# Four small reorderings in a linear-attention and token-mixer kernel: the opening's statistics and transposes, one fill and one sum in the first mixer, one sum in the second

## The chip, the cores and the metric

The kernel runs on one core of one Trainium2 chip. The metric is the device time of one execution in microseconds (us), lower is better. A ratio is the mean time of one kernel's fast runs over the mean of the other's fast runs of the same rounds, so it is not quite the ratio of the medians quoted beside it.

## The reference, cut to what matters

```python
x = A_x                                            # 2048 tokens x 1024, bf16
h  = x + linear_attention(layernorm(x), wqkv, wo)  # 32 heads of 32
h2 = h + mixer(layernorm(h), w1, b1, w2, b2)       # per feature: 2048 -> 3584 -> gelu -> 2048
```

Three stretches matter here. In the **opening** the first four tiles of 128 tokens are loaded, normalised, transposed on TensorE and multiplied with the key weights. The **first mixer** is the product with w1, the **second mixer** that with w2. Both mixers are computed with seven half-size products in place of eight (a Strassen-like scheme, applied twice: seven outer products "p1" to "p7", some of them split again into seven inner ones "i1" to "i7"). The scheme costs many sums and differences of operands on VectorE and copies on ScalarE; TensorE's stream is meant never to wait for them. Each mixer goes through its outputs in **quads**, four tiles of 128 at a time; "in2", "in3" and "in5" are the inner blocks of p2, p3 and p5, and "hi", "wq", "e" are tiles that VectorE's sums write.

## The kernel before

The order on each engine is mostly the order of the program. The opening, with lines that the change doesn't touch cut:

```python
pin(ln[0][1](0)); warm_up(2, ...)      # statistics of tile 0, first half; warm-up matmuls
pin(ln[0][1](1)); pin(ln[0][2]())      # second half, aggregate
warm_up(2, ...)
stats(0)                               # ScalarE: 1/sqrt(var)
norm_halves(0)                         # VectorE: normalise tile 0
transpose_in(0)                        # TensorE: 2 x 4 transposes; ScalarE: 2 copies 128x512
ln_stats(1); stats(1)                  # statistics of tile 1
k_unit(0, 0)                           # 8 products 128x512 with key weights
norm_halves(1); transpose_in(1)
ln_stats(2); stats(2); k_unit(1, 0); norm_halves(2)
# ... k_unit(0, 1), transpose_in(2), ln_stats(3), stats(3)
phi_dve((0, 0))
w_sums(kmov, slice(0, 1))              # VectorE: 1.22 us sum of weights
norm_halves(3)
# ... k_unit(1, 1)
transpose_in(3)
```

Both mixers weave the seven inner products with steps of an outer one; each stretch of such steps is a **fill**:

```python
def interleave(self, n, steps, at={}, flush=...):
    t = len(steps)
    cuts = [0, (5*t+8)//16, (9*t+8)//16, (12*t+8)//16, t]
    for f in (n.i1, "b", 0, n.i6, "c", n.i2, "2", 1, n.i5, n.i7, "7", 2, n.i3, "third", 3, n.i4, "end"):
        ...   # a number: that share of the steps; a string: flush late ScalarE work, run at[name]
```

An inner block keeps two halves, b and c (and a and e), of PSUM banks. In the second mixer b and c are halves of one bank. i7 adds into c and VectorE then reads c; i3 adds into b. In the second mixer the sums for p7 stood together ahead of the block:

```python
self.asums(7)                          # two sums wq<-wq, one for each of the pair
self.interleave(self.in5, self.steps(*[st.p6 for st in sts]))
third_sums()                           # only in the first quad: four more sums
```

Of the kernel before, what the change touches and what calls it, by code (L numbers as in the profile page):

```python
# [30 lines left out]
def kernel(  # L31
# [62 lines left out]
    def warm_up(n, behind=None):  # L94
        def mm(lhsT, rhs):
            ps = warm_tiles[0]
            warm_tiles.append(warm_tiles.pop(0))
            pin(nc.tensor.matmul(ps[0:lhsT.shape[-1], 0:rhs.shape[-1]], lhsT=lhsT, rhs=rhs, start=True, stop=True))

        if behind is not None:  # L100
            mm(behind, behind)
        for t in range(n):
            mm(warm[:, 0:P], warm[:, 0:BANK])
# [395 lines left out]
    class Quad:  # L499
# [27 lines left out]

        late = []

        def interleave(self, n, steps, at={}, flush=(("7", None), ("end", None))):  # L530
            t = len(steps)
            cuts = [0, (5 * t + 8) // 16, (9 * t + 8) // 16, (12 * t + 8) // 16, t]
            flush = dict(flush)

            def fill(q):
                for f, part in groupby(steps[cuts[q]:cuts[q + 1]], lambda s: s[0]):
                    f([k for _, k in part], self.late)

            def point(name):
                todo = len(self.late) if flush.get(name, 0) is None else flush.get(name, 0)  # L540
                for _ in range(todo):
                    self.late.pop(0)()
                at.get(name, nop)()

            for f in (
                n.i1, "b", 0, n.i6, "c", n.i2, "2", 1, n.i5, n.i7, "7", 2, n.i3, "third", 3, n.i4, "end",
            ):
                if isinstance(f, int):
                    fill(f)
                elif isinstance(f, str):  # L550
                    point(f)
                else:
                    f()
# [25 lines left out]
        def run2(self, pend, on_p4, on_p7, cut, third_sums):  # L579
            sts = self.sts  # L580

            def starting():
                self.in1.sums(slice(2, 4))
                self.asums(5)
                self.in5 = self.inner(5)
                self.in5.sums(slice(0, 2))
                sts[0].asum(6)
                for st in sts:
                    st.begin()

            self.interleave(
                self.in1, self.steps(*[st.p4 for st in pend]),
                {"b": starting, "7": lambda: self.in5.sums(slice(2, 4))}, (("b", self.early), ("7", None), ("end", None)),
            )
            sts[1].asum(6)
            on_p4()
            e = share(sts)
            for st in sts:
                st.fetch(1, 1)
            for st in sts:  # L600
                st.fetch(0, 0)
                st.fetch(0, 1)
            self.asums(7)
            self.interleave(self.in5, self.steps(*[st.p6 for st in sts]))
            third_sums()
            self.asums(3)
            in3 = Inner2(sts, 3, self.mov3, "i", self.add_to(e), None)
            in3.sums()
            for st in sts:
                st.p7()  # L610
                dve.tensor_tensor(st.e[:], st.B[:], st.e[:], ALU.add)
            if cut is not None:
                sts[-1].split(cut)
            for st in sts:
                st.fetch(1, 0)
            nxt, halves = on_p7()

            def begin_next():
                if nxt is not None:
                    nxt.in1 = nxt.inner(1)  # L620
                    nxt.in1.sums(slice(0, 2))
                sts[0].evac(0, 1, sts[0].e)

            self.interleave(in3, self.steps(*[st.p2 for st in sts]), {
                "2": halves[0], "7": halves[1], "third": begin_next,
                "end": lambda: self.late.append(lambda: sts[1].evac(0, 1, sts[1].e)),
            }, (("7", None),))
            return sts, nxt
# [43 lines left out]
        def run1(self, pend, nxt, on_p4, third_sums=None):  # L672
            sts = self.sts
            s4, s6, s7 = self.steps(*[st.p4 for st in pend]), self.steps(*[st.p6 for st in sts]), self.steps(*[st.p7_fill for st in sts])
            c6, c7 = 3 * len(s6) // 4, len(s7) // 2

            def starting():
                self.in1.sums(slice(2, 4))
                self.asums(5)
                self.in5 = Inner(sts, 5, self.mov5, "i5", self.sink5, self.sum5)  # L680
                self.in5.sums(slice(0, 2))
                self.asums(6)
                self.t1 = self.base("t1a")
                for s, st in enumerate(sts):
                    st.begin(self.t1[:, s, :])

            def gelu(s, dh, t):
                return lambda: sts[s].evac(0, dh, t[:, s, :])

            def gelu_late(*args):  # L690
                return lambda: self.late.insert(0, gelu(*args))

            self.in1.behind = self.late
            self.interleave(
                self.in1, s4, {"b": starting, "7": lambda: self.in5.sums(slice(2, 4))}, (("b", None), ("7", None))
            )
            self.asums(7)
            in2 = Inner2(sts, 2, self.mov2, "i1", self.add_to(self.t1), None)
            in2.sums()
            on_p4()  # L700
            nxt = nxt()
            share(sts)
            if third_sums is not None:
                third_sums(slice(0, 3))
            self.interleave(self.in5, s6[:c6], flush=(("b", None), ("7", None), ("end", None)))
            sts[0].finish()
            self.asums(3)
            self.base3()
            in3 = Inner2(sts, 3, self.mov3, "i5", self.add_to(self.t3), None)
            in3.sums()  # L710
            sts[0].with_shared(sts[0].base3, sts[0].B)
            self.interleave(
                in2, s6[c6:] + s7[:c7], {"third": gelu(0, 0, self.t1), "end": gelu_late(1, 0, self.t1)}, (("7", None),)
            )
            sts[1].with_shared(sts[1].base3, sts[1].B)
            if nxt is not None:
                nxt.begin1()
            self.interleave(in3, s7[c7:], {
                "7": nop if third_sums is None else lambda: third_sums(slice(3, 4)),
                "third": gelu(0, 1, self.t3), "end": gelu_late(1, 1, self.t3),  # L720
            }, (("b", 1), ("c", None)))
            return sts, nxt
# [13 lines left out]
    with ExitStack() as actx:  # L736
# [21 lines left out]
        with ExitStack() as a1:  # L758
# [28 lines left out]
            def ln_chunks(i, x_sb):  # L787
                st = a1s.tile([P, NDC, nc.vector.BN_STATS_DIM], F32, name="st")
                mv = a1s.tile([P, nc.vector.BN_AGGR_DIM], F32, name="mv")
                lnv = a1s.tile([P, 1], F32, name="lnv")  # L790
                rstd = a1s.tile([P, 1], F32, name="rstd")
                xn = xin.tile([P, D], BF16, name="xn")

                def stats(c):
                    return nc.vector.bn_stats(st[:, c, :], x_sb[:, c * CW:(c + 1) * CW])

                def aggr():
                    return nc.vector.bn_aggr(mv[:], st[:])

                def scale():  # L800
                    yield nc.scalar.activation(lnv[:], mv[:, 1:2], ACT.Ln, bias=eps_ln[:], scale=1.0)
                    yield nc.scalar.activation(rstd[:], lnv[:], ACT.Exp, scale=-0.5)

                def norm(cs):
                    return nc.vector.tensor_scalar(xn[:, cs], x_sb[:, cs], mv[:, 0:1], rstd[:, 0:1], ALU.subtract, ALU.mult)

                return xn, stats, aggr, scale, norm, st, mv
# [264 lines left out]
            def stats(i):  # L1072
                for op in ln[i][3]():
                    pin(op)
# [28 lines left out]
                phis[i, c] = k_parts(i, c)  # L1103

            phis = {}
            warm_up(2, xs[0][:, 0:CW // 8])
            ln[0] = ln_chunks(0, xs.pop(0))
            pin(ln[0][1](0))
            warm_up(2, ln[0][5][:, 0, :])
            pin(ln[0][1](1))  # L1110
            pin(ln[0][2]())
            warm_up(2, ln[0][6][:])
            stats(0)
            norm_halves(0)
            transpose_in(0)
            ln_stats(1)
            stats(1)
            k_unit(0, 0)
            norm_halves(1)
            transpose_in(1)  # L1120
            ln_stats(2)
            stats(2)
            k_unit(1, 0)
# [541 lines left out]
```

## Time and profile before

| | before |
|---|---|
| time, median of 3 runs | 566.08 us (565.63 to 566.12) |
| span of the profiled execution | 564.1 us |
| TensorE busy | 555.1 us (98%) |
| share of the chain of waits that is TensorE | 91% |

The head of the page of the kernel before, and the fourth part of it (the chain that ended last):

```profile
span 564.1 us, 8722 instructions
PE 555.1 (98%) x3262; PEld 310.0 (55%) x3278; DVE 448.3 (79%) x853; ACT 287.4 (51%) x609; POOL 1.8 (0%) x8
...
PE 91%; DVE 6%; ACT 1%; issue 1%; DVEq 0%
```

TensorE is the bound, so only its gaps can be won. The list of TensorE's waits in the kernel before (who waited for whom: us in total, times, longest):

```profile
PE psI L229 <- DVE e L229: 1.9, 3, 0.7
...
PE acc_t L826 <- ACT xnT L1079: 0.9, 2, 0.5
PE psI L229 <- DVE hi L229: 0.4, 1, 0.4
...
```

The opening in the timeline (columns: start, duration, engine, line, operation, written <- read, shape, count; in brackets the idle time before it and what ended it):

```profile
10.50 3.63 PE L826 MATMUL acc_t<-wkv,xnT 128*128 128x512 bf16 x15 [0.46 <-ACT xnT L1079]
...
12.06 1.29 DVE L795 BATCH_NORM_STATS2 st<-x_sb 128x6 f32<-128x512 bf16 x2
...
13.97 0.61 PE L1069 MATMUL tp<-ident,xn 128*128 128x128 bf16 x8
14.20 1.22 DVE L876 TENSOR_TENSOR pqT<-wkv 128x2048 f16<-128x2048 bf16 x1
...
15.92 0.73 DVE L805 TENSOR_SCALAR xn<-x_sb,mv,rstd 128x512 bf16<-128x512 bf16 x2 [0.51 <-ACT rstd L802]
16.39 0.72 PE L1069 MATMUL tp<-ident,xn 128*128 128x128 bf16 x8
```

The product group at 10.50 is tile 1's key unit, which waited for ScalarE's copy (tile 0's, at 7.70, did likewise); the transposes (tp) at 13.97 and 16.39 are tile 2's and tile 3's, 2.42 us apart. Those of tile 3 come right behind tile 3's normalisation; pqT<-wkv is the weight sum.

The first mixer, one quad, in the timeline:

```profile
268.32 0.35 ACT L229 COPY psI<-psI 128x256 f32<-128x256 f32 x1
268.73 0.60 PE L229 MATMUL psI<-hi,is 128*128 128x256 f16 x4
...
272.63 0.60 PE L229 MATMUL psI<-hi,wq 128*128 128x256 f16 x4
...
277.23 0.68 DVE L229 TENSOR_TENSOR hi<-hO,hi 128x1024 f16<-128x1024 f16 x1
...
277.97 0.60 PE L229 MATMUL psI<-hi,sa 128*128 128x256 f16 x4 [0.39 <-DVE hi L229]
```

The product at 268.73 starts just as ScalarE's copy of 268.32 is over; the product at 277.97 waits for the sum "hi".

The second mixer, first of three quads:

```profile
449.54 2.08 DVE L229 TENSOR_TENSOR wq<-wq 128x1792 f16<-128x1792 bf16 x2
...
451.54 0.42 DVE L229 TENSOR_TENSOR e<-psI,es 128x256 f32<-128x256 f32 x1
452.01 0.93 PE L229 MATMUL psI<-gE,is 128*128 128x256 f16 x7 [0.65 <-DVE e L229]
...
452.97 0.42 DVE L229 TENSOR_TENSOR e<-psI,es 128x256 f32<-128x256 f32 x1 [1.01 <-PE psI L229]
```

Both sums wq<-wq run ahead of the addition that the product at 452.01 needs.

### The profile page before, as it was taken

The page shows a single profiled execution, that of the slowest core. Times are in us where ns is not written, and L with a number is a line of the kernel's source. Part 1 is how long each engine was busy: PE and PEld are TensorE (multiplying, and loading weights), DVE is VectorE, ACT ScalarE, POOL GpSimd, SP SyncE. Part 2 cuts the span into 40 slices and gives each one's busy share as a digit, 9 for nine tenths or more (in the row PEclk, how much of TensorE's full clock was granted, in tenths as well). Part 3 has the DMA queues.
Part 4 walks back from the last instruction along what each step waited for, and adds up shares of the span by engine and source line. Part 5 has one row for each costly group of instructions (what it writes and reads, how often), then busy time and mean ns, then how long its engine had stood idle before and what let it go on. Part 6 is the DMA issues. An engine that isn't in the chain of part 4 may idle for free.

```text
span 564.1 us, 8722 instructions
## 1 busy us (share of the span) xinstructions
PE 555.1 (98%) x3262; PEld 310.0 (55%) x3278; DVE 448.3 (79%) x853; ACT 287.4 (51%) x609; POOL 1.8 (0%) x8
## 2 busy tenths in 40 slices
PE   8999999999999999999999999999999999999997
PEld 3444444454444444456666766666445656656654
DVE  6898888544776788889889789888998899869874
ACT  4747777766766877645546465555211313213212
POOL 1000000000000000000000000000000000000000
PEclk9999999999999999999999999999999999999999
DMA  9933342115764861103041340432946643652111
GB/s 303 295 76 75 79 90 39 19 50 193 216 207 130 251 189 74 74 1 127 25 149 35 116 150 1 150 79 53 246 131 183 168 113 117 182 147 79 56 38 56
DMA packets 86218, 67.15 MB, mean 119 GB/s; under 512 B 15891, under 2 KB 80161, under 8 KB 86177
## 3 DMA queue, kind: packets, MB, share of 16 engines
q1 hardware_dynamic: 85440, 65.94, 39.9%
q10 hardware_dynamic: 672, 0.66, 0.3%
q8 instruction: 25, 0.41, 0.3%
q14 instruction: 17, 0.13, 0.1%
q0 software_dynamic: 64, 0.01, 0.0%
HBM read 54.54 MB, written 8.91 MB: 112 GB/s over the span
## 4 chain that ended last, share of the span: by engine, by line
PE 91%; DVE 6%; ACT 1%; issue 1%; DVEq 0%
PE psI L229 20%; PE acc_t L229 18%; PE psC L229 15%; PE psB L229 6%; PE psA L229 4%; PE psC L902 4%; PE psB L902 4%; PE psA L902 4%; DVE gs L229 3%; PE acc_t L826 3%; PE psB L341 2%; PE psA L341 2%; PE acc_t L1177 2%; PE psE L902 2%; PE psC L341 2%; PE kvps L855 1%
## 5 line engine op out<-in xcount | busy, mean ns | idle before, releaser
L229 PEld LDWEIGHTS <-is 128*128 128x128 f16 x652 | 63.7, 98 | 31.6 <-issue 4.0
L229 PEld LDWEIGHTS <-sa 128*128 128x128 f16 x606 | 59.3, 98 | 28.5 <-issue 0.7
L229 PEld LDWEIGHTS <-wq 128*128 128x128 bf16 (+1 forms) x503 | 49.2, 98 | 32.6
L229 PE MATMUL acc_t<-wo_sb,pqT 128*128 128x512 f16 x256 | 55.6, 379 | 0.0
L229 PE MATMUL acc_t<-xnT,wq_sb 128*128 128x512 bf16 x188 | 43.1, 379 | 0.2
L229 PEld LDWEIGHTS <-pqT 128*128 128x128 bf16 x256 | 25.0, 98 | 30.5 <-issue 0.6
L191 DVE TENSOR_SCALAR e_sb<-e_sb 128x512 bf16<-128x512 bf16 x64 | 18.6, 290 | 28.7 <-ACT e_sb L187 28.1
L187 ACT ACTIVATE e_sb<-acc_t 128x512 bf16<-128x512 f32 x40 | 23.9, 597 | 24.6 <-PE acc_t L229 12.0
L902 PEld LDWEIGHTS <-xs 128*128 128x128 f16 x208 | 20.0, 98 | 23.4 <-DVE xs L888 1.3
L229 PE MATMUL psC<-gs,wq 128*128 128x512 f16 x140 | 32.0, 379 | 0.0
L229 PE MATMUL psC<-hT,sa 128*128 128x512 f16 x112 | 31.2, 379 | 0.0
L229 PEld LDWEIGHTS <-wq_sb 128*128 128x128 bf16 x192 | 18.5, 98 | 23.0 <-issue 1.3
L229 PE MATMUL psI<-hi,is 128*128 128x256 f16 x200 | 30.0, 272 | 0.0
L229 PE MATMUL psB<-hT,sa 128*128 128x512 f16 x112 | 29.7, 379 | 0.0
L229 DVE BATCH_NORM_STATS2 hst<-acc_t 128x6 f32<-128x512 f32 x32 | 21.4, 693 | 9.0 <-ACT h_bf L229 8.9
L902 PE MATMUL psA<-wkv,xnT 128*128 128x512 bf16 x98 | 26.0, 379 | 0.3
L902 PEld LDWEIGHTS <-xnT 128*128 128x128 bf16 x156 | 15.2, 98 | 18.5 <-issue 0.2
L229 PE MATMUL psC<-hT,wq 128*128 128x512 f16 x96 | 24.6, 379 | 0.0
L229 ACT CAST h_bf<-acc_t 128x512 bf16<-128x512 f32 x32 | 18.4, 581 | 11.9 <-PE acc_t L229 11.6
L188 ACT ACTIVATE r_sb<-acc_t 128x512 bf16<-128x512 f32 x40 | 23.7, 593 | 0.0
L229 ACT COPY psI<-psI 128x256 f32<-128x256 f32 x50 | 17.9, 359 | 11.2 <-PE psI L229 9.9
L826 PE MATMUL acc_t<-wkv,xnT 128*128 128x512 bf16 x94 | 21.5, 379 | 1.0 <-ACT xnT L1079 0.9
(223 smaller groups left out, 1075.5 us busy)
## 6 DMA issues: line engine op xcount, KB each, us to landing
wq<-in_B_w_dram SPq DMA_DIRECT2D x14, 1024.0 KB, 7.8
wq<-in_B_w_dram SPq DMA_DIRECT2D x12, 896.0 KB, 6.5
xr<-in_A_x_dram SPq DMA_DIRECT2D x16, 256.0 KB, 4.9
rdb<-rd_dram SPq DMA_DIRECT2D x32, 128.0 KB, 4.0
h_dram<-h_bf SPq DMA_DIRECT2D x16, 256.0 KB, 2.0
hr<-h_dram SPq DMA_DIRECT2D x32, 128.0 KB, 3.2
out_dram<-ot SPq DMA_DIRECT2D x31, 128.0 KB, 1.9
x_sb<-in_A_x_dram SPq DMA_DIRECT2D x15, 256.0 KB, 3.0
```

The source lines that it names most:

```text
L187: pin(nc.scalar.activation(e_sb[:], src, ACT.Exp))
L188: pin(nc.scalar.activation(r_sb[:], src, ACT.Relu))
L191: pin(nc.vector.tensor_scalar(e_sb[:], e_sb[:], 1.0, PHI_EPS, ALU.min, ALU.add))
L229: return (lambda *a, **kw: pin(op(*a, **kw))) if self.always or getattr(Held, self.key) else op
L341: pe.matmul(ps[:, cols], lhsT=lhs[:, k, :], rhs=mv(k)[:, cols], start=(start and k == 0), stop=(k == self.nk - 1), skip_group_check=True,)
L826: mm = nc.tensor.matmul(pp[:, 0:CW], lhsT=xnT[:, kt, i * P:(i + 1) * P], rhs=wkv[:, kt, c * CW:(c + 1) * CW], start=(kt == 0), stop=(kt == ...
L855: pin(nc.tensor.matmul(kv_ps[b][:, sl, :], lhsT=pks[i % NPK][:, j * P:(j + 1) * P], rhs=vaugs[i % NVA][:, j, :], start=False, stop=(i == N ...
L902: pin(nc.tensor.matmul(ps[:], lhsT=lhs[:, k, :], rhs=rhs[:, k, :], start=(start and k == 0), stop=(k == hk2 - 1), skip_group_check=True,))
L1177: nc.tensor.matmul(qp[:, 0:SW], lhsT=wq_sb[:, kt, j * P:(j + 1) * P], rhs=xnT[:, kt, u * SW:(u + 1) * SW], start=(kt == 0), stop=(kt == ND ...
```

## The change

Its intent: (1) use VectorE's idle time in the opening for tile 1's statistics, copy the first half of each transposed tile in two pieces, and put tile 1's transposes inside the first key unit; (2) shift one fill in the first mixer forward (`first=1`); (3) move one sum of the third block ("hi") into an earlier idle time of VectorE; (4) put the second pair's seventh sum behind the two additions.

```diff
-        def interleave(self, n, steps, at={}, flush=(("7", None), ("end", None))):
+        def interleave(self, n, steps, at={}, flush=(("7", None), ("end", None)), first=0):
             t = len(steps)
-            cuts = [0, (5 * t + 8) // 16, (9 * t + 8) // 16, (12 * t + 8) // 16, t]
+            cuts = [0, (5 * t + 8) // 16 + first, (9 * t + 8) // 16 + first, (12 * t + 8) // 16 + first, t]
@@ second mixer, run2
-            self.asums(7)
+            sts[0].asum(7)
             self.interleave(self.in5, self.steps(*[st.p6 for st in sts]))
+            sts[1].asum(7)
             third_sums()
@@ first mixer, run1
+            def before_gelu():
+                if third_sums is not None:
+                    third_sums(slice(3, 4))
+                gelu(0, 0, self.t1)()
-            self.interleave(self.in5, s6[:c6], flush=(("b", None), ("7", None), ("end", None)))
+            self.interleave(self.in5, s6[:c6], flush=(("b", None), ("7", None), ("end", None)), first=1)
-                in2, s6[c6:] + s7[:c7], {"third": gelu(0, 0, self.t1), "end": ...
+                in2, s6[c6:] + s7[:c7], {"third": before_gelu, "end": ...
             self.interleave(in3, s7[c7:], {
-                "7": nop if third_sums is None else lambda: third_sums(slice(3, 4)),
@@ opening (cut)
+            def transpose_first(i, k0, k1):
+                dst, tp = transpose_half(i, 0)
+                for q in range(0, hk, 2):
+                    pin(nc.scalar.copy(dst[:, q:q + 2, :], tp[:, q:q + 2, :]))
+                if k0:
+                    phis[0, 0] = k_parts(0, 0, range(k0, k1))
+                pin(nc.scalar.copy(*transpose_half(i, 1)))
-            warm_up(2, ln[0][5][:, 0, :])
+            warm_up(1, ln[0][5][:, 0, :])
-            warm_up(2, ln[0][6][:])
+            warm_up(1, ln[0][6][:])
             stats(0)
+            pin(ln[1][1](0))
             norm_halves(0)
-            transpose_in(0)
-            ln_stats(1)
+            transpose_first(0, 0, 0)
+            pin(ln[1][1](1))
+            pin(ln[1][2]())
             stats(1)
-            k_unit(0, 0)
+            k_parts(0, 0, range(0, 6))
             norm_halves(1)
-            transpose_in(1)
+            transpose_first(1, 6, ND)
```

More of the change, by code (lines that the diff above doesn't have):

```diff
@@ L712, in run1 @@
             self.interleave(
-                in2, s6[c6:] + s7[:c7], {"third": gelu(0, 0, self.t1), "end": gelu_late(1, 0, self.t1)}, (("7", None),)
+                in2, s6[c6:] + s7[:c7], {"third": before_gelu, "end": gelu_late(1, 0, self.t1)}, (("7", None),)
             )
@@ L1105 @@
             phis = {}
+            def transpose_first(i, k0, k1):
[5 more added lines that the diff above has]
+                pin(nc.scalar.copy(*transpose_half(i, 1)))
             warm_up(2, xs[0][:, 0:CW // 8])
-            ln[0] = ln_chunks(0, xs.pop(0))
+            for i in range(2):
+                ln[i] = ln_chunks(i, xs.pop(i))
             pin(ln[0][1](0))
-            warm_up(2, ln[0][5][:, 0, :])
+            warm_up(1, ln[0][5][:, 0, :])
             pin(ln[0][1](1))
             pin(ln[0][2]())
-            warm_up(2, ln[0][6][:])
+            warm_up(1, ln[0][6][:])
             stats(0)
+            pin(ln[1][1](0))
             norm_halves(0)
-            transpose_in(0)
-            ln_stats(1)
+            transpose_first(0, 0, 0)
+            pin(ln[1][1](1))
+            pin(ln[1][2]())
             stats(1)
-            k_unit(0, 0)
+            k_parts(0, 0, range(0, 6))
             norm_halves(1)
-            transpose_in(1)
+            transpose_first(1, 6, ND)
             ln_stats(2)
```

## The prediction

> **What bounds it now.** TensorE. The page's first part has it busy 98% of a 564.1 us span; the chain of waits is 91% TensorE. So only TensorE's idle gaps can be won. From the timeline (group starts against 0.216 us per 512-column product) and the list of waits:
> - Opening: until 13.9 us TensorE follows tile 0 and tile 1 through statistics, normalisation, transpose and copy. First key product at 7.70, tile 1's at 10.50, each after a 0.45 us wait for ScalarE's 128x512 copy (about 0.54 apart).
> - First mixer, six quads: the second inner product of in2 waits 0.08 to 0.09 us for ScalarE's copy in front of it, which stands behind the copies of e and psC; once, at 277.97, it waits 0.39 for the vector sum "hi".
> - Second mixer, three quads (452.0, 493.0, 534.1): TensorE waits 0.65 for VectorE's addition e<-psI,es, 1.9 in total. Two 1.04 us sums (wq<-wq) stand before it. The waiting product writes the other half of the same PSUM bank; the Trainium skill (PSUM — Partial Sum Buffer, "PSUM bank collisions raise a hardware error") says two engines must not touch one bank and quadrant together, and the trace agrees: the product starts 0.05 after the 0.42 us addition ends.
>
> **What changes** (order of instructions; DMA order is the same).
> 1. VectorE does one 0.64 us half of tile 1's statistics while ScalarE makes tile 0's scale (0.60 idle there now), so tile 0's normalisation slips by at most 0.1 us. The first half of each transposed tile is copied in two 256-column pieces (estimate 0.36 each, as other 128x256 ScalarE copies), so the first key product starts about 0.2 earlier per tile. Two warm-up matmuls go. Six of eight products of unit (0,0) run before tile 1's transposes and two between the halves, hiding the copy. I get: first product near 7.2; tile 1's normalisation still near 8.5 (its scale now queues behind ScalarE's copies); tile 1's key unit near 9.9 instead of 10.50. Gain 0.55. Inputs land in time (x1 at 4.5, second key weights by 11.4); later vector work follows TensorE, so it is kept.
> 2. first=1 finishes the first p6 one fill earlier: the psC copy moves ahead, the copy before in2's second product is no longer late. 6 x 0.085 = 0.5.
> 3. The sum hi<-hO,hi moves into VectorE's 0.60 idle at 272.7. Gain 0.39.
> 4. With one wq sum behind the additions, the addition can run about 1.04 earlier and ends before the fill does; the wait goes: 3 x 0.65 = 1.95. The moved sum is needed only some 3 us later.
>
> Sum 3.4 us, all on the critical path.
>
> **Prediction** 562.7 us, range 561.9 to 564.0. Faster by over 2%: 0.01; within 2%: 0.98; slower: 0.01.
>
> **What would show it.** TensorE's waits for e at the second mixer gone (1.9 to under 0.2), the wait for hi gone, in2 gaps gone, unit (1,0) at about 9.9 us.
>
> **What would make it wrong.** The clock: 512-column matmuls start 0.41 us apart until about 6.1 us and 0.22 after. The Trainium skill (TensorE: Matmul & The Clock Gate, "What's actually happening") explains this by a window of activity of about 3.4 us. With fewer warm-ups the full rate may come later and cost 0.5 to 1.5 us. Or tile 1's scale arrives late behind the three copies; or in the first second-mixer quad (extra sums of gO) VectorE, now 0.4 us later, delays the third product's sums.

## The result

| | before | after |
|---|---|---|
| time, median of 4 runs | 566.10 us (565.63 to 566.31) | 563.14 us (563.09 to 563.61) |
| ratio, 95% interval | | 0.9951 (0.9934 to 0.9968) |
| span of the profiled execution | 564.1 us | 561.8 us |

The kernel is 2.96 us faster by the medians. The profiled execution of after is the slowest of its four (563.61), so its trace shows only 2.3 us of it. The changed kernel, run again in five rounds (label r1_after_again below), gave 563.65 and 0.9958. All outputs are right.

The page's head, and TensorE's waits after:

```profile
span 561.8 us, 8720 instructions
PE 554.2 (99%) x3260; PEld 309.7 (55%) x3276; DVE 447.8 (80%) x853; ACT 288.5 (51%) x611; POOL 1.8 (0%) x8
```

```profile
...
PE tp L1074 <- DVE xn L810: 1.0, 1, 1.0
PE psI L229 <- DVE e L229: 0.5, 2, 0.3
PE acc_t L831 <- DMA wkv<-in_A_wqkv_dram: 0.3, 1, 0.3
...
```

The waits that the change aimed at are gone (hi, ScalarE's xnT, three times e). Three others are new: 1.0 us before transposes in the opening, 0.3 for the load of key weights, and 0.5 in all for an addition "e", two times, at another place than before.

The same product is found in both traces, so start-before less start-after says how far the changed kernel is ahead at each point. The pieces between the points are what each part brought:

| point (start in the trace of before) | ahead by | what lies between |
|---|---|---|
| tile 2's transposes, 13.97 us | 0.97 | opening, first part |
| tile 3's transposes, 16.39 us | 0.08 | opening, second part: lost again |
| first inner product of the first mixer, 241.67 us | 0.08 | nothing |
| product after the moved "hi", 277.97 us | 0.67 | one quad of `first`, +0.03; hi, +0.56 |
| first inner product of the second mixer, 431.45 us | 0.82 | the other five quads of `first` |
| waiting product of the first quad, 452.01 us | 1.64 | +0.82 |
| next quad's first inner product, 472.48 us | 0.66 | lost again, -0.98 |
| waiting product of the third quad, 534.07 us | 2.29 | two more times +0.81 |

The opening after, in the timeline, from tile 1's key unit on:

```profile
9.55 3.62 PE L831 MATMUL acc_t<-wkv,xnT 128*128 128x512 bf16 x15
...
12.58 1.29 DVE L800 BATCH_NORM_STATS2 st<-x_sb 128x6 f32<-128x512 bf16 x2 [0.81 <-DMA x_sb<-in_A_x_dram]
13.00 0.61 PE L1074 MATMUL tp<-ident,xn 128*128 128x128 bf16 x8
14.71 1.22 DVE L881 TENSOR_TENSOR pqT<-wkv 128x2048 f16<-128x2048 bf16 x1
15.84 0.73 DVE L810 TENSOR_SCALAR xn<-x_sb,mv,rstd 128x512 bf16<-128x512 bf16 x2
16.31 0.72 PE L1074 MATMUL tp<-ident,xn 128*128 128x128 bf16 x8 [0.97 <-DVE xn L810]
```

Tile 1's key unit starts at 9.55 against 10.50, tile 2's transposes at 13.00 against 13.97. Then TensorE waits 0.97 us: VectorE's statistics of tile 3 waited 0.81 us for tile 3's load, and the weight sum still stands between them and the normalisation.

The first mixer after:

```profile
267.89 0.36 ACT L229 COPY psI<-psI 128x256 f32<-128x256 f32 x1
268.56 0.60 PE L229 MATMUL psI<-hi,is 128*128 128x256 f16 x4
...
272.52 0.60 PE L229 MATMUL psI<-hi,wq 128*128 128x256 f16 x4
272.71 0.68 DVE L229 TENSOR_TENSOR hi<-hO,hi 128x1024 f16<-128x1024 f16 x1
...
277.30 0.60 PE L229 MATMUL psI<-hi,sa 128*128 128x256 f16 x4
```

ScalarE's copy of 267.89 is over 0.3 us before the product that needs it. But the product psI<-hi,wq is ahead by 0.11 only, where the one at 268.56 was by 0.17. A narrow window of the same trace names the cause:

```profile
272.04 0.76 DVE L229 TENSOR_TENSOR t1a<-psI,t1a 128x256 f32<-128x256 f32 x2
272.52 0.49 PE L229 MATMUL psI<-hi,wq 128*128 128x256 f16 x3
```

The first of these two additions lasts 0.42 us, to 272.46, and reads the half bank that the product at 272.52 adds into. The additions run 0.13 us later than before (the pair started at 271.91 there), because the extra fill puts i3 of the preceding block 0.13 later and VectorE's queue follows in order.

The second mixer after, first quad:

```profile
448.71 1.08 DVE L229 TENSOR_TENSOR wq<-wq 128x1792 f16<-128x1792 bf16 x1
449.71 0.42 DVE L229 TENSOR_TENSOR e<-psI,es 128x256 f32<-128x256 f32 x1
450.37 0.93 PE L229 MATMUL psI<-gE,is 128*128 128x256 f16 x7
451.34 0.42 DVE L229 TENSOR_TENSOR e<-psI,es 128x256 f32<-128x256 f32 x1 [1.21 <-PE psI L229]
451.68 1.08 DVE L229 TENSOR_TENSOR wq<-wq 128x1792 f16<-128x1792 bf16 x1
...
467.16 1.24 DVE L229 TENSOR_TENSOR e<-psI,e 128x512 f32<-128x512 f32 x2
468.45 0.93 PE L229 MATMUL psI<-gO,is 128*128 128x256 f16 x7 [0.32 <-DVE e L229]
...
471.06 0.92 PE L229 MATMUL psI<-gi,sa 128*128 128x256 f16 x7 [0.17 <-DVE e L229]
```

The aimed wait is gone, but VectorE now idles 1.21 us between the additions and does the second sum only then. In this quad, which also has the four third_sums, it stays late, and some 17 us on TensorE waits for its additions at 468.45 and 471.06.

### The profile page after: what moved, and what is told of

It is laid out like the page before. It is cut to its first block, busy times and chain, and to the rows that moved or that the text cites. A ratio compares the mean times of both kernels' runs of the same rounds, so it can differ in the third digit from the quotient of the medians.

```text
span 561.8 us, 8720 instructions
## 1 busy us (share of the span) xinstructions
PE 554.2 (99%) x3260; PEld 309.7 (55%) x3276; DVE 447.8 (80%) x853; ACT 288.5 (51%) x611; POOL 1.8 (0%) x8
## 4 chain that ended last, share of the span: by engine, by line
PE 91%; DVE 5%; DMA 2%; issue 1%; SPq 1%; ACT 0%; DVEq 0%
PE psI L229 21%; PE acc_t L229 18%; PE psC L229 14%; PE psB L229 8%; PE psC L907 4%; PE psB L907 4%; PE psA L907 4%; PE psA L229 3%; PE psB L341 2%; PE psA L341 2%; PE acc_t L1193 2%; PE psE L907 2%; PE psC L341 2%; PE acc_t L831 2%; DMA x_sb<-in_A_x_dram 2%; PE kvps L860 1%
```

## The experiments

All kernels were timed in five rounds against the kernel before, in three calls, each on one chip: r1, e3, e4, e7; then e1, e5, e6, e2; then e8, e9, e10. Across calls only the ratios should be compared.

### r1_after_again: the changed kernel again

No edit; it shares the chip with the next three.

> The changed kernel itself, so that the next three have it on the same chip. Both theories: 2.5 to 3.2 us under the kernel before (first measured: 2.96). If the third tile's load is what takes the opening's gain, then in this profile VectorE's fourth statistics (tile 3) either wait for that load, and tile 3's transposes start near 16.3 us, or find it landed, and they start before 15.9 us; the run time follows, 0.4 to 0.6 us apart.

Measured: 563.65 us median (563.32 to 563.85), ratio 0.9958 (0.9945 to 0.997). In its profile the statistics of tile 3 start at 12.80 us, after a wait of 0.31 for the load, and tile 3's transposes at 16.53, so this is the late case, somewhat later than expected. But in this execution most of the lead was lost earlier, to another load: TensorE's first key product waited 1.3 us for its key weights.

```profile
8.33 1.46 PE L831 MATMUL acc_t<-wkv,xnT 128*128 128x512 bf16 x6 [1.30 <-DMA wkv<-in_A_wqkv_dram]
```

Tile 1's key unit starts at 10.50 us and tile 2's transposes at 13.95, level with the kernel before; between tile 2's and tile 3's transposes only 0.15 us more is lost (0.89 in the trace of after). This profile is of the slowest of the five runs; what the other four did in the opening is not known.

### e3_sum7_between: the seventh sum between the additions

```diff
-            self.interleave(self.in5, self.steps(*[st.p6 for st in sts]))
-            sts[1].asum(7)
+            self.interleave(self.in5, self.steps(*[st.p6 for st in sts]), {"7": lambda: sts[1].asum(7)})
```

> The second pair's seventh sum stands between the two additions instead of behind both. My theory: the 0.97 us that the first second-mixer quad gave back (0.15 + 0.49 + 0.33 between 465 and 471 us) came from VectorE running about 1 us later, because it stood idle 1.21 us between the additions and did the sum after them. Then that idle time takes the 1.04 us sum, the waits of TensorE for the addition at 468 and 471 go, the first product of the quad gains about 0.8 as before, and the kernel is 0.8 to 1.0 us under the changed kernel. Rival: the give-back comes from TensorE alone being 0.8 us earlier against sums that are bound elsewhere (loads of w2, output stores); then the waits stay and the time moves by less than 0.3 us.

Measured: 562.58 us, ratio 0.9938 (0.9925 to 0.995), 1.07 us under r1 by the medians. The timeline of its first quad:

```profile
449.65 0.42 DVE L229 TENSOR_TENSOR e<-psI,es 128x256 f32<-128x256 f32 x1
449.99 1.08 DVE L229 TENSOR_TENSOR wq<-wq 128x1792 f16<-128x1792 bf16 x1
450.31 0.93 PE L229 MATMUL psI<-gE,is 128*128 128x256 f16 x7
451.28 0.42 DVE L229 TENSOR_TENSOR e<-psI,es 128x256 f32<-128x256 f32 x1 [0.21 <-PE psI L229]
...
467.75 0.93 PE L229 MATMUL psI<-gO,is 128*128 128x256 f16 x7
...
470.03 0.93 PE L229 MATMUL psI<-gi,sa 128*128 128x256 f16 x7
```

The sum takes the idle time (1.21 left to 0.21), and the two later waits are gone. TensorE's lead over the kernel before grows by 0.81 in each of the three quads and gives nothing back. VectorE's lateness was the cause; the rival (other bounds) is out.

### e4_wsum_later: the weight sum behind tile 3's normalisation

```diff
-            w_sums(kmov, slice(0, 1))
             norm_halves(3)
+            w_sums(kmov, slice(0, 1))
```

> The first weight sum of the keys (1.22 us on VectorE) is put behind tile 3's normalisation. My theory: the opening wins 0.95 us up to tile 2's transposes (13.00 against 13.97), and loses it before tile 3's because VectorE does that normalisation only after the weight sum, its statistics having waited 0.81 us for the load of tile 3. With the sum behind, tile 3's transposes start at 15.2 to 15.5 us instead of 16.31 and the kernel is 0.5 to 0.9 us under the changed kernel. Rival: the load of tile 3 alone decides it, and the order of VectorE does nothing: tile 3's transposes stay at 16.0 to 16.4 us, the time within 0.2 us of the changed kernel's.

Measured: 562.70 us (562.4 to 563.02, all five under all five of r1), ratio 0.9942 (0.9928 to 0.9955), 0.95 under r1. Tile 3's transposes start at 15.45 us. But tile 3's load came early in this profile (statistics at 11.76, no wait), and 11.76 + 3.73, the distance of the changed kernel, is 15.49: the profile fits the rival as well. The times seem to speak for the order, but r1 is a poor measure of it: its profile had lost the lead to the key weights before the weight sum could matter (at tile 2's transposes 0.01 us in hand, 0.94 in e4). So neither tells. e9 was made for that. What ends last before tile 3's normalisation is now ScalarE's scale:

```profile
14.98 0.73 DVE L810 TENSOR_SCALAR xn<-x_sb,mv,rstd 128x512 bf16<-128x512 bf16 x2 [1.00 <-ACT rstd L807]
```

### e7_both: both moves

The edits of e3 and e4 together.

> Both of the moves. If the two causes are separate, their gains add: 1.3 to 1.9 us under the changed kernel, near 561.5 us. If they compete for the same slack, the gain is that of the larger one alone, 0.8 to 1.0 us.

Measured: 561.74 us (561.4 to 562.0), ratio 0.9924 (0.9911 to 0.9936), 1.91 under r1, where e3 and e4 gave 1.07 and 0.95 alone. The two causes are separate: in its trace nothing is given back in the second mixer, and nothing is lost between tile 2's and tile 3's transposes.

### e1_sum7_only, e5_first_only, e6_hi_only, e2_opening_only: one part each on the kernel before

Each holds the lines of its part of the diff above and nothing else.

> Only the seventh sum's move, on the kernel before. My theory: three waits of 0.81 us (start to start) go and the first quad gives 0.97 back, so 1.4 to 1.5 us under the kernel before, and the waits for the addition near 469 and 472 us appear. Rival: the give-back needs the other parts of the change; then 2.2 to 2.5 us under.

Measured: 564.54 us against 565.66, ratio 0.9978 (0.9966 to 0.9991). Between its first and last waiting product TensorE gains 0.82, loses 0.97 by 472 us, then gains 0.81 twice: 1.46 in sum, and the two waits for the addition are there (0.5 us). The part gives back by itself; the rival (2.2 to 2.5 us) is out. By the medians it is 1.12 us, under the expected 1.4 to 1.5; the interval (about 0.5 to 1.9 us) holds both, and the profiled run came 0.21 us behind out of the opening, which this part doesn't touch.

> Only first=1. My theory: each of the six in2 loses its wait of 0.085 us before the second product, and hands 0.055 back before the fourth product (which waits for VectorE); 0.03 a quad, 0.15 to 0.2 in all, hard to see in the time but plain in the starts of the products. Rival (the prediction's): 0.5 us.

Measured: 565.50 us, ratio 0.9999 (0.9987 to 1.0012): nothing to be seen in the time. In the starts of the products it gains 0.20 us over the six quads, each time +0.08 to +0.09 at i6, the block's second product, and -0.05 to -0.07 at i4, its last (the "fourth product" of the expectation).

> Only the fourth sum of the third block (hi) moved forward. My theory: the product at 277.97 us starts 0.55 us earlier, as in the changed kernel, and keeps it: 0.5 to 0.6 us under the kernel before. Rival (the prediction's size, from the list of waits): 0.39 us.

Measured: 565.41 us, ratio 0.9993 (0.998 to 1.0005): inconclusive in the time. In the trace the product of 277.97 us gains 0.56 (from 0.23 behind to 0.33 ahead) and keeps it.

> Only the opening. My theory: tile 1's key unit starts 0.6 to 0.95 us earlier, but what is left at 31 us (start of the first value product) depends on tile 3's load: 0.1 us left where the fourth statistics wait for it, 0.5 to 0.6 where they do not; in the median 0.3 to 0.6 us under the kernel before. Rival: the two warm-up matmuls that were taken out delay the full clock, and the opening gains nothing or loses: 0 to 1 us over.

Measured: 565.22 us (565.11 to 566.46), ratio 0.9996 (0.9982 to 1.001), 0.44 by the medians; the interval holds nothing and the expected gain alike. In its profile tile 3's statistics start at 12.00 us after a load wait of 0.47, its transposes at 15.73, and the first mixer is 0.66 ahead. So the loss is not in the taking out of warm-ups: the lead is still 1.13 us at tile 2's transposes and falls to 0.66 only before tile 3's, long after the full rate was reached. That rate came between about 4.5 and 6.9 us in the nine profiles of the changed opening and between about 5.6 and 6.7 in the four of the old one. Where it came last (e8 and e9) most of tile 0's eight transposes ran 0.11 us apart in place of 0.055, and the lead at the first key product was 0.38 us against 0.84 in the trace of after; so a late rate may move the opening by tenths. Whether fewer warm-ups make it later is not shown: they were not varied alone.

### e8_x3_early: tile 3's load one place earlier

```diff
             for k0 in (0, hk):
                 nc.sync.dma_start(wkv[:, k0:k0 + hk, CW:D], ...)
-            for i in range(3, G0 + 2):
+                if k0 == 0:
+                    xs[3] = load_x(3)
+            for i in range(4, G0 + 2):
```

> The changed kernel with the load of tile 3 issued one place earlier (before the second half of the second key weights). In all profiles of the changed opening so far tile 3's transposes start 3.73 us after its statistics start (12.58 to 16.31, 12.80 to 16.53, 12.52 to 16.25, 12.00 to 15.73). If the load sets those statistics, they start at 11.6 to 11.9 us here, the transposes at 15.3 to 15.6, and the kernel is 0.4 to 0.9 us under the changed kernel's 0.9958 of the kernel before. Rival: the weight half that now lands later holds TensorE before tile 2's transposes, and nothing is gained.

Measured: 562.99 us (562.66 to 563.02), ratio 0.9947 (0.9934 to 0.9959). Statistics at 11.91 us without a wait, transposes at 15.73, slightly later than expected, because TensorE itself was later here (tile 2's transposes at 13.30 against 13.00 in after). From there to tile 3's it is 2.43 us, as before the change: nothing is lost. The load is one of the two things that set this wait, and the weights that now land later cost nothing visible.

### e9_wsum_later_x3_late: the sum later, the load late on purpose

The edit of e4, and `for i in (4, 3, 5): xs[i] = load_x(i)` for the order of loads.

> The weight sum behind tile 3's normalisation, as in e4, and the load of tile 3 issued behind tile 4's, so that it lands late on purpose. In e4's profile the load came early (statistics at 11.76 us), so it did not tell the two theories apart. If the weight sum's place matters, transposes start 2.8 to 2.9 us after the statistics (1.29 statistics, 0.24 aggregate, about 0.8 scale, 0.4 normalisation); if it does not, 3.7 as before. The time itself will be worse than e4's: the statistics at 13 us or later.

Measured: 562.99 us (562.65 to 563.03), ratio 0.9946 (0.9934 to 0.9959). Its timeline:

```profile
12.94 1.29 DVE L800 BATCH_NORM_STATS2 st<-x_sb 128x6 f32<-128x512 bf16 x2 [0.94 <-DMA x_sb<-in_A_x_dram]
...
15.26 0.73 DVE L810 TENSOR_SCALAR xn<-x_sb,mv,rstd 128x512 bf16<-128x512 bf16 x2
15.72 0.72 PE L1074 MATMUL tp<-ident,xn 128*128 128x128 bf16 x8
15.90 1.22 DVE L881 TENSOR_TENSOR pqT<-wkv 128x2048 f16<-128x2048 bf16 x1
```

The load is later than in any other profile, and still the transposes start 2.78 us after the statistics, where four profiles of the changed opening had 3.73; with 3.73 they would have started at 16.67. They follow tile 2's (13.30) by 2.42 us, where after, with an earlier load, took 3.31. The order on VectorE matters by itself. That the time would be clearly worse than e4's was not so: the late load landed only a little later than the unlucky ones.

### e10_both_x3_early: e7 with the load earlier

> e7 (seventh sum between the additions, weight sum later) with tile 3's load one place earlier. If the load and the weight sum act on the same wait, e7 has already taken what there is, and this is within 0.3 us of e7's 0.9924 of the kernel before. If they are separate, another 0.4 us or more.

Measured: 561.75 us, ratio 0.9927 (0.9914 to 0.9941), level with e7's 0.9924. The load and the sum act on the same wait; either cure takes it. In all five kernels with one cure or both (e4, e7, e8, e9, e10) tile 3's transposes start 2.42 or 2.43 us after tile 2's, the distance of the kernel before. There the next limit stands, which the traces of e4 and e7 name: ScalarE makes tile 3's scale only behind its two copies of tile 2. The best versions are e7 and e10, both below the changed kernel.

## Why the prediction was right, and where its terms were off

The total was right: 562.7 predicted, 563.14 and 563.65 measured, within 561.9 to 564.0. The bound (TensorE) was right too, and each of the four moves did remove the wait that it aimed at. None of the four sizes was right, and the errors partly cancel. In the trace of after, the opening brought 0.08 where 0.55 was put and the fill 0.18 where 0.5 was; hi brought 0.56 for 0.39 and the three additions 2.44 for 1.95; and 0.97 was given back. That makes 2.29 us, where 3.4 was predicted: that the total came within the range is in part luck.

1. "Six times 0.085 = 0.5" for the fill came to 0.18 in the trace of after and 0.20 alone (e5). The 0.085 was won in every quad, but some 0.055 was handed back at the last product of the block, where VectorE's addition became the last thing to end. The prediction asked only what the copy's wait would do.
2. "Gain 0.39" for hi came to 0.56, and "3 x 0.65" to three times 0.81. Both were read from the idle time in the list of waits. That idle time begins when the preceding product ends by the model, and a 128x512 product takes 379 ns where products follow each other every 216. The Trainium skill (TensorE: Matmul & The Clock Gate, "Single matmul latency") has a constant of 166 ns for that part of a warm product that isn't streaming; this trace agrees with 379 - 216 = 163, though the trace's end of a product is itself modelled. What is measured is the starts: an idle time of 0.39 or 0.65 stood for a loss of 0.56 or 0.81, about 0.16 more. The prediction had the starts of the groups in view too and took the shorter numbers.
3. "Sum 3.4 us, all on the critical path" left out the return of 0.97 us in the first second-mixer quad. The prediction had named it as the last of its risks, without a size. e1 shows that it belongs to that part alone, e3 that it was 1 us of VectorE's idle time between the two additions.
4. "Gain 0.55" for the opening: in the trace of after tile 1's key unit started even before it was expected (9.55 against 9.9 us), and 0.97 us was in hand at tile 2's transposes. "Inputs land in time", "so it is kept" is the step that failed. What was left at the first value product (the psA<-wkv group) can be read from four profiles with the old opening (31.00, 31.21, 30.81, 31.23; mean 31.06) and four with the new (30.92, 31.14, 30.87, 30.34; mean 30.82): 0.24 us, with a spread of the same size. The rest was lost in two places. Between tile 2's and tile 3's transposes the four lost 0.89 (after), 0.15 (r1), 0.73 (e3) and 0.47 us (e2): tile 3's load, taken as landed, held the statistics in all four, and the weight sum stood in VectorE's queue between them and the normalisation. In r1 nearly all had gone before, while TensorE waited 1.3 us for the first unit's key weights, a load that the prediction doesn't list (after lost 0.3 us to it). With the sum moved behind (e4, e7, e9, e10) or the load earlier (e8) nothing is lost between the two transposes, and the first value product is at 30.06, 30.29, 30.34, 30.05 and 30.34.

The feared 0.5 to 1.5 us from a late full rate did not show in the times; what the traces show of it stands under e2. The reading of the PSUM wait held: with the addition over at 450.13 us, the product starts at 450.37 without a wait for it.

What stays open: why tile 3's load, issued at the same place in the same order, lets the statistics start anywhere from 11.76 to 12.80 us. The traces narrow it down. In all ten profiles with the loads in the same order it lands 4.33 to 4.39 us after the second half of the first unit's key weights, and that half lands anywhere from 7.12 (e7) to 8.38 us (r1). So the lateness is already there with the key weights, and tile 3's load inherits it. Why the key weights land early or late was not pursued; no run here moved them, so an execution of e7 may lose time to them, as r1's did.

## What to carry to other kernels

Read the worth of a gap on a pipelined TensorE from start to start, not from the idle time that the list of waits gives. Moving work behind a needed operation of an engine that takes its work in order (VectorE here idled 1.21 us ahead of the moved sum) is only half of the job: put it into a known idle time of that engine (here between two additions that both wait on TensorE), or the engine is late for what comes next. When an opening is made faster, look at the next input and at whatever postponable work stands between its landing and its use.

## What the Trainium skill lacked or had wrong

- TensorE: Matmul & The Clock Gate and Perfetto Trace Analysis: neither says that the idle time before a TensorE instruction understates what the wait costs. Here idle times of 0.39 and 0.65 us cost 0.56 and 0.81.
- PSUM — Partial Sum Buffer ("PSUM bank collisions raise a hardware error") gives the rule for whose sake a product is made to wait for a read of the other half of its bank. It has no cost for such a wait; here it was 0.81 us, three times, and the product followed the end of the addition by 0.05 us.
